# Seven rounds of token routing beside the big products: one scaled running value per token, token-by-expert blocks made once a round, longer gaps

## The chip, the core and the metric

The kernel runs on one core of one Trainium2 chip. The core has a matrix engine (PE, with a second row PEld for its weight loads), a vector engine (DVE), an activation engine (ACT), a general engine (POOL) and a queue that issues DMAs (SP). They run side by side and wait for each other through semaphores; each works through its own instructions in the order in which the program holds them. The metric is the time of one execution on the device in microseconds (us), the median of several runs.

## The reference

Three stages follow each other: a gated linear attention (4 batches, 8 heads, 768 steps, head size 48), a dense layer of 384 to 2048 and back for 3072 tokens, and a routed layer of 8 experts. The change lies in the last one, in the choice of the tokens of each expert:

```
logits = x @ w_gate                       # 3072 tokens x 8 experts
order = np.argsort(-flat)                 # all 24576 pairs, greatest first
for idx in order:
    tok, e = (int(idx) // E, int(idx) % E)
    if assigned[tok] >= 0 or counts[e] >= cap:   # cap = 3072 / 8 = 384
        continue
    assigned[tok] = e; counts[e] += 1
for e in range(E):
    mask = assigned == e
    out[mask] = np.maximum(x[mask] @ w1[e], 0.0) @ w2[e]
```

## The kernel before

The tokens lie as 24 columns of 128. The dense layer is done in groups of three columns: `first` makes `hp` (384 to 2048) and `second` makes `xp` (back to 384). The last three groups' `second` is kept for the end of the program, because the routing needs all logits and these can be had without it: 9 columns of 48 big products, 432 in all, each 128x128 by 128x384, written `xp`. Behind them come 8 experts of 144 big products each: 72 written `hp` (8 blocks of 9) and 72 written `yp` (3 columns of 24). This is `layer2`, the stage of which the change moves the work.

Beside these products runs `route()`. The greedy choice is made in seven rounds, one for each expert that fills up. In a round every token that is still free has its best open expert, and the question is which expert fills first, and at which logit. The logit is turned into a whole number (`key`), and its 32 bits are searched in seven levels, from the top digit down: 5, 5, 5, 5, 4, 4 and 4 bits, that is 32 or 16 thresholds a level. One level is a chain between DVE and PE:

- DVE makes `dg` (the digit plus one), `ge` (token's digit at least each threshold, 768 columns for 32 thresholds, 384 for 16) and `oh` (a block of 128 x 8 x 24: does this token still run, with this expert).
- PE counts, in `c`: `ge` times `oh`, 6 small products for 32 thresholds and 3 for 16. DVE picks the diagonal (`cm`) and sums it (`cd`); PE spreads it over the partitions (`cnt`); DVE compares with the room left (`ok`); PE sums over the experts by powers of two (`tot`); DVE counts the thresholds that some expert still fills (`scr`, with `J`, the digit found, as its running sum).
- With `J` DVE narrows `oh` and `v` to the tokens of that digit, adds to `abv` the tokens above it, and takes their number (`cg`) from the room (`kr`).

In the kernel before, `dg`, `ge` of the next level do not depend on `J`; they are made ahead, `ge` in two halves. Only `scr` and `oh` stand between `tot` and the next `c`.

Behind the seven levels a round has a tail: the expert found is written off, `ps` (two small products) numbers its tokens, and the next round's `m`, `eq0`, `key`, `am`, `oh` and `ge` are made. `token_list` turns the numbers into lists of rows: `ohs`, `h12` and `rh` on DVE, then `pi` and `pj` on PE, then `idx` and `row`, by which POOL gathers the tokens (`xg`) and writes the results (`out`).

The order of the instructions is set in two steps. A driver writes the program: big products advance a clock by their 160 ns each, and a side job runs on when its gap has passed; `GAP` holds the routing's gaps. Then a scheduler of the framework places each engine's instructions by its own costs, so the number of big products between two small ones is not the gap divided by 160. `high_priority` marks the evictions of the big products: `x2` behind `xp` (DVE and ACT), and behind an expert's `hp` the halves `hh` (ACT) and `hl`, in turn on POOL (even blocks) and DVE (odd blocks). All instructions are recorded by one helper, so every row of the trace bears the line L84 and is told by its tile.

Of the kernel before, what the change touches and what calls it, by code (L numbers as in the profile page):

```python
# [9 lines left out]
F32 = mybir.dt.float32  # L10
F16 = mybir.dt.float16
BF16 = mybir.dt.bfloat16
# [79 lines left out]
def body(tc, qk, v, f_logit, w_in, w_out, w_gate, w1, w2, out):  # L92
# [20 lines left out]
    with ExitStack() as ctx:  # L113
# [513 lines left out]
        LEVELS = [(27, 5), (22, 5), (17, 5), (12, 5), (8, 4), (4, 4), (0, 4)]  # L627
        R = {}

        def route_constants():  # L630
# [59 lines left out]

            DVE.tensor_copy(const("opn", [128, E]), wd)
# [13 lines left out]
        def route():  # L705
# [6 lines left out]
            for rnd in range(E - 1):  # L712
# [12 lines left out]
                di = small([128, len(LEVELS), NT], "di", I32)  # L725

                def digit(l):
                    sh, w = LEVELS[l]
                    DVE.tensor_scalar(di[:, l, :], key, sh, 2 ** w - 1, op0=OP.logical_shift_right, op1=OP.bitwise_and)

                def at_least(l):

                    w = LEVELS[l][1]
                    T, G = 2 ** w, 128 >> w
                    dg = small([128, NT], "dg", BF16, 3)
                    DVE.tensor_scalar(dg, di[:, l, :], 1.0, None, op0=OP.add)
                    ge = small([128, NT * 32], "ge", BF16)[:, :NT * T].rearrange("p (a t g) -> p a t g", t=T, g=G)
                    da = dg.rearrange("p (a g) -> p a g", g=G)[:, :, None, :].to_broadcast([128, NT // G, T, G])
                    h = NT // G // 2

                    def part(b):
                        DVE.tensor_tensor(ge[:, b], da[:, b], R[f"thr{w}"][:, b], op=OP.is_ge)

                    return dg, ge, part, (slice(0, h), slice(h, NT // G))

                digit(0)

                oh = small([128, E, NT], "oh", BF16, 3)
                DVE.tensor_tensor(oh, wdx, am[:, None, :].to_broadcast([128, E, NT]), op=OP.is_equal)
                dg, ge, part, halves = at_least(0)  # L750
                part(slice(0, NT // (128 >> LEVELS[0][1])))
                v = small([128, NT], "v", BF16, 3)
                DVE.tensor_tensor(v, dg, un, op=OP.mult)
                kr, abv, cnt, J = kcap, None, None, None
                for l, (sh, w) in enumerate(LEVELS):
                    T, G = 2 ** w, 128 >> w
                    if l > 0:
                        kr, abv = count_above()
# [597 lines left out]
```

## Time and profile before

| what | value |
|---|---|
| three runs | 813.64, 815.62 and 816.38 us, median 815.62 |
| the profiled execution | 822.74 us, its span 820.9 |
| PE busy | 755.0 us (92%), granted clock 0.974 |
| DVE busy | 580.5 us (71%), 1879 instructions |
| ACT, POOL busy | 357.4 us, 142.2 us |

A big product takes a slot of about 0.16 us on PE although its bar is twice as long, since the products are pipelined; so a busy PE hides short waits, and the starts of the instructions say more than the bars. The idle time that a row puts before a product starts at the end of the bar in front of it, some 0.17 us later than the end of that product's slot.

### The profile page before, as it was taken

What the parts mean: (1) busy time and instruction counts of PE and PEld (TensorE: products, weight loads), DVE (VectorE), ACT (ScalarE), POOL (GpSimd) and SP (SyncE); (2) the same over time, 40 slices, a digit from 0 to 9 for tenths busy, and PEclk for the clock granted to TensorE, in tenths of its full rate; (3) what the DMA queues carried; (4) which work ended last, traced back from release to release, by engine and by line L of the source; (5) the groups of instructions that cost most, each with busy time, mean ns of one, the idle gap of its engine ahead of it and who ended that gap; (6) DMA issues with size and microseconds to landing.
All of it is one profiled execution on the core that took longest, in us unless ns stands there. A gap on an engine that the chain in (4) does not pass through costs nothing.

```text
span 820.9 us, 15764 instructions
## 1 busy us (share of the span) xinstructions
PE 755.0 (92%) x5927; PEld 497.6 (61%) x5927; DVE 580.5 (71%) x1879; ACT 357.4 (44%) x748; POOL 142.2 (17%) x140
## 2 busy tenths in 40 slices
PE   6888999899898898989999999999979988989996
PEld 5856776666576565747666666555545545556663
DVE  6799988767975876796673466999899889821310
ACT  6567657655854764583461354000122222213320
POOL 5345311000000000000000000010253443453111
PEclk9699899999999998999999999999999999999998
DMA  9965545698898998996553100040375764744200
GB/s 242 239 155 165 161 128 136 170 276 277 279 270 285 283 296 249 264 324 194 94 96 70 33 1 2 21 174 25 99 239 168 176 182 134 225 155 179 97 30 29
DMA packets 111646, 135.92 MB, mean 166 GB/s; under 512 B 62929, under 2 KB 94674, under 8 KB 109522
## 3 DMA queue, kind: packets, MB, share of 16 engines
q1 hardware_dynamic: 106194, 100.31, 45.2%
q0 software_dynamic: 5376, 34.61, 12.3%
q8 instruction: 46, 0.75, 0.4%
q14 instruction: 30, 0.25, 0.1%
HBM read 86.52 MB, written 34.60 MB: 148 GB/s over the span
## 4 chain that ended last, share of the span: by engine, by line
PE 47%; DVE 24%; DMA 9%; issue 9%; ACT 5%; SPq 5%; POOL 1%; POOLq 0%; ACTq 0%; DVEq 0%
PE hp L84 16%; PE xp L84 13%; DMA xw_s<-in_moe_w 8%; PE yp L84 7%; SPq L84 5%; DVE winu L84 3%; PE y L84 3%; DVE xw_l L84 2%; DVE g L84 2%; PE P L84 2%; DMA fT<-in_f_logit 1%; PE A L84 1%; ACT xw_h L84 1%; PE U L84 1%; DVE woutu L84 1%
## 5 line engine op out<-in xcount | busy, mean ns | idle before, releaser
L84 PE MATMUL hp<-xT,winh 128*128 128x384 f16 x768 | 192.3, 330 | 16.2 <-DVE g L84 16.0
L84 PE MATMUL xp<-wo,gh 128*128 128x384 f16 x768 | 192.1, 328 | 3.1 <-ACT wo L84 2.9
L84 PE MATMUL hp<-xT,winl 128*128 128x384 f16 x384 | 126.6, 330 | 0.0
L84 PE MATMUL xp<-wo,gl 128*128 128x384 f16 x384 | 125.8, 328 | 0.0
L84 PEld LDWEIGHTS <-winh 128*128 128x128 f16 x768 | 74.3, 99 | 64.1 <-issue 24.6
L84 PEld LDWEIGHTS <-gh 128*128 128x128 f16 x912 | 84.2, 98 | 44.4 <-issue 2.9
L84 PE MATMUL hp<-x2T,w1e 128*128 128x384 f16 x576 | 99.7, 325 | 0.8 <-ACT x2T L84 0.6
L84 PE MATMUL yp<-w2e,hh 128*128 128x384 f16 x384 | 95.2, 325 | 0.0
L84 DVE SCALAR_TENSOR_TENSOR xw_l<-xw_s,xw_h 128x768 f16<-128x768 f32 x64 | 61.1, 955 | 46.3 <-ACT xw_h L84 45.8
L84 ACT ACTIVATE g<-hp 128x384 f32<-128x384 f32 x152 | 73.0, 484 | 22.4 <-PE hp L84 20.0
L84 ACT ACTIVATE xw_h<-xw_s 128x768 f16<-128x768 f32 x64 | 53.8, 841 | 65.6 <-DMA xw_s<-in_moe_w 62.7
L84 DVE SCALAR_TENSOR_TENSOR g<-hp,g 128x384 f32<-128x384 f32 x128 | 70.2, 551 | 12.7 <-ACT g L84 12.3
L84 PEld LDWEIGHTS <-w1e 128*128 128x128 f16 x576 | 53.8, 97 | 34.9 <-issue 1.6
L84 PEld LDWEIGHTS <-gl 128*128 128x128 f16 x528 | 48.9, 97 | 31.9 <-issue 4.4
L84 ACT ACTIVATE gh<-g 128x768 f16<-128x768 f32 x64 | 53.8, 841 | 27.4 <-DVE g L84 27.3
L84 DVE TENSOR_TENSOR gl<-g,gh 128x768 f16<-128x768 f32 x52 | 49.7, 955 | 21.5 <-ACT gh L84 21.3
L84 PE MATMUL yp<-w2e,hl 128*128 128x384 f16 x192 | 62.5, 325 | 2.3 <-issue 2.3
L84 POOL IOTA jp<- 128x128 f32 x2 | 0.5, 238 | 369.5 <-PE hp L84 369.4
L84 ACT ACTIVATE hh<-hp 128x384 f16<-128x384 f32 x64 | 31.4, 491 | 72.4 <-PE hp L84 64.3
L84 DVE SCALAR_TENSOR_TENSOR hl<-hp,hh 128x384 f16<-128x384 f32 x40 | 22.1, 553 | 51.6 <-ACT hh L84 49.1
L84 PEld LDWEIGHTS <-winl 128*128 128x128 f16 x384 | 38.0, 99 | 23.2 <-issue 1.4
L84 ACT ACTIVATE x<-yp 128x384 f32<-128x384 f32 x24 | 11.8, 491 | 92.1 <-PE yp L84 89.2
(266 smaller groups left out, 1309.2 us busy)
## 6 DMA issues: line engine op xcount, KB each, us to landing
xw_s<-in_moe_w SPq DMA_DIRECT2D x64, 384.0 KB, 5.3
qkT<-in_qk SPq DMA_DIRECT2D x48, 192.0 KB, 3.6
wout_s<-in_moe_w_out SPq DMA_DIRECT2D x16, 384.0 KB, 3.0
w1d<-xw_h SPq DMA_DIRECT2D x32, 192.0 KB, 3.4
w1d<-xw_l SPq DMA_DIRECT2D x32, 192.0 KB, 4.6
w2d<-xw_h SPq DMA_DIRECT2D x32, 192.0 KB, 4.6
w2d<-xw_l SPq DMA_DIRECT2D x32, 192.0 KB, 4.3
fT<-in_f_logit SPq DMA_DIRECT2D x24, 192.0 KB, 4.2
```

The source lines that it names most:

```text
L84: i = f(*args, **kwargs)
```

## The change

- Levels: 5, 5, 5, 5, 5, 4 and 3 bits with 32, 32, 32, 32, 32, 16 and 16 thresholds, where there were four levels of 32 and three of 16.
- One running value `v` per token takes the place of `oh`, `kr` and `abv` of each level: `v = (v - J) + dg`, with each level's digits scaled by a power of two (`STEP`), so that a token whose digit was above `J` stays above all thresholds of the later levels, and one below stays below. `oh` is made once a round, `ok` compares with `kcap`, and `cg` and `abv` are made once, behind the last level.
- All later digits of a round are made together, in three instructions on blocks of 128 x 144 (`di` shifted, `di` masked, `dg` scaled), instead of two small ones a level.
- `ge` of a level compares `v` with that level's thresholds (`thl1` to `thl6`, made once at the start on DVE, while POOL fills the 18 rows of `sh`, `mk` and `unit`). It now needs `J`, and is one instruction of 768 or 384 columns.
- `GAP` goes from (1000, 500, 500, 700, 1200) to (1500, 700, 600, 700, 2000).

The core of the diff:

```diff
-        LEVELS = [(27, 5), (22, 5), (17, 5), (12, 5), (8, 4), (4, 4), (0, 4)]
+        LEVELS = [(27, 5, 32), (22, 5, 32), (17, 5, 32), (12, 5, 32), (7, 5, 32), (3, 4, 16), (0, 3, 16)]
+        STEP = [2.0 ** (-6 * l) for l in range(len(LEVELS))]
...
+            n = len(LEVELS) - 1
+            sh, mk = (const(x, [128, n, NT], I32) for x in ("sh", "mk"))
+            unit = const("unit", [128, n, NT])
+            for l, (s, w, T) in enumerate(LEVELS[1:]):
+                POOL.memset(sh[:, l, :], s)
+                POOL.memset(mk[:, l, :], 2 ** w - 1)
+                POOL.memset(unit[:, l, :], STEP[l + 1])
+            R["thr"] = [R["thr5"]]
+            for l, (s, w, T) in enumerate(LEVELS):
+                if l > 0:
+                    t = R["thr5" if T == 32 else "thr4"]
+                    u = rc.tile(list(t.shape), BF16, name=f"thl{l}")
+                    DVE.tensor_scalar(u, t, STEP[l], None, op0=OP.mult)
+                    R["thr"].append(u)
+            DVE.tensor_scalar(const("i1s", [128, 16]), R["i1"][:, :16], STEP[-1], None, op0=OP.mult)
...
-                di = small([128, len(LEVELS), NT], "di", I32)
-                def digit(l):
-                    sh, w = LEVELS[l]
-                    DVE.tensor_scalar(di[:, l, :], key, sh, 2 ** w - 1, op0=OP.logical_shift_right, op1=OP.bitwise_and)
-                def at_least(l):
-                    w = LEVELS[l][1]
-                    T, G = 2 ** w, 128 >> w
-                    dg = small([128, NT], "dg", BF16, 3)
-                    DVE.tensor_scalar(dg, di[:, l, :], 1.0, None, op0=OP.add)
+                v = small([128, NT], "v", BF16, 3)
+                d0 = small([128, NT], "d0", I32)
+                DVE.tensor_scalar(d0, key, LEVELS[0][0], 2 ** LEVELS[0][1] - 1, op0=OP.logical_shift_right, op1=OP.bitwise_and)
+                oh = small([128, E, NT], "oh", BF16)
+                DVE.tensor_tensor(oh, wdx, am[:, None, :].to_broadcast([128, E, NT]), op=OP.is_equal)
+                DVE.scalar_tensor_tensor(v, d0, 1.0, un, op0=OP.add, op1=OP.mult)
+                for l, (sh, w, T) in enumerate(LEVELS):
+                    G = 128 // T
                     ge = small([128, NT * 32], "ge", BF16)[:, :NT * T].rearrange("p (a t g) -> p a t g", t=T, g=G)
-                    da = dg.rearrange("p (a g) -> p a g", g=G)[:, :, None, :].to_broadcast([128, NT // G, T, G])
-                    h = NT // G // 2
-                    def part(b):
-                        DVE.tensor_tensor(ge[:, b], da[:, b], R[f"thr{w}"][:, b], op=OP.is_ge)
-                    return dg, ge, part, (slice(0, h), slice(h, NT // G))
-                digit(0)
-                oh = small([128, E, NT], "oh", BF16, 3)
-                DVE.tensor_tensor(oh, wdx, am[:, None, :].to_broadcast([128, E, NT]), op=OP.is_equal)
-                dg, ge, part, halves = at_least(0)
-                part(slice(0, NT // (128 >> LEVELS[0][1])))
-                v = small([128, NT], "v", BF16, 3)
-                DVE.tensor_tensor(v, dg, un, op=OP.mult)
-                kr, abv, cnt, J = kcap, None, None, None
-                for l, (sh, w) in enumerate(LEVELS):
-                    T, G = 2 ** w, 128 >> w
-                    if l > 0:
-                        kr, abv = count_above()
-                    more = l + 1 < len(LEVELS)
-                    if more:
-                        digit(l + 1)
-                        dg2, ge2, part, halves = at_least(l + 1)
+                    va = v.rearrange("p (a g) -> p a g", g=G)[:, :, None, :].to_broadcast([128, NT // G, T, G])
+                    DVE.tensor_tensor(ge, va, R["thr"][l], op=OP.is_ge)
+                    if l == 0:
+                        di = small([128, len(LEVELS) - 1, NT], "di", I32)
+                        DVE.tensor_tensor(di, key[:, None, :].to_broadcast([128, len(LEVELS) - 1, NT]), R["sh"], op=OP.logical_shift_right)
+                        DVE.tensor_tensor(di, di, R["mk"], op=OP.bitwise_and)
+                        dg = small([128, len(LEVELS) - 1, NT], "dg", BF16)
+                        DVE.scalar_tensor_tensor(dg, di, 1.0, R["unit"], op0=OP.add, op1=OP.mult)
                     yield GAP[0] if l else GAP[4]
                     c4 = bank([128, E, G], "c4")
                     for a in range(NT // G):
                         mm(c4, ge[:, a], oh[:, :, a * G:(a + 1) * G], a == 0, a == NT // G - 1)
+                    wt = T.bit_length() - 1
                     cm = small([128, E * 8], "cm", F16)[:, :E * G].rearrange("p (e g) -> p e g", g=G)
-                    DVE.tensor_tensor(cm, c4, R[f"diag{w}"], op=OP.mult)
+                    DVE.tensor_tensor(cm, c4, R[f"diag{wt}"], op=OP.mult)
                     cd = R[f"cd{l % 2}"]
                     with nc.allow_low_precision("one count and zeros"):
                         DVE.tensor_reduce(cd[:, :E], cm, axis=AX.X, op=OP.add)
-                    if more:
-                        part(halves[0])
                     yield GAP[1]
                     cnt = bank([128, 32], "cnt")
-                    mm(cnt[:, :T], cd, R[f"sel{w}"], True, True)
+                    mm(cnt[:, :T], cd, R[f"sel{wt}"], True, True)
                     ok = small([128, 32], "ok", BF16)
-                    DVE.tensor_scalar(ok[:, :T], cnt[:, :T], kr, None, op0=OP.is_ge)
-                    if more:
-                        part(halves[1])
+                    DVE.tensor_scalar(ok[:, :T], cnt[:, :T], kcap, None, op0=OP.is_ge)
                     yield GAP[2]
                     tot = bank([128, 32], "tot")
                     mm(tot[:, :T], R["bits"], ok[:, :T], True, True)
                     J = small([128, 1], "J")
                     scr = small([128, 32], "scr")
-                    DVE.tensor_scalar(scr[:, :T], tot[:, :T], 1.0, None, op0=OP.is_ge, op1=OP.add, accum_out=J)
-                    vp = v
-                    if more:
-                        op = oh
-                        oh = small([128, E, NT], "oh", BF16, 3)
-                        DVE.scalar_tensor_tensor(oh, dg[:, None, :].to_broadcast([128, E, NT]), J, op,
-                                                 op0=OP.is_equal, op1=OP.mult)
-                        dg, ge = dg2, ge2
+                    DVE.tensor_scalar(scr[:, :T], tot[:, :T], STEP[l], None, op0=OP.min, op1=OP.add, accum_out=J)
+                    if l + 1 < len(LEVELS):
+                        vp = v
                         v = small([128, NT], "v", BF16, 3)
-                        DVE.scalar_tensor_tensor(v, vp, J, dg, op0=OP.is_equal, op1=OP.mult)
-                    def count_above(vp=vp, J=J, cnt=cnt, kr=kr, abv=abv, T=T):
-                        cg, k2 = small([128, 1], "cg"), small([128, 1], "kr", F32, 3)
-                        s8 = small([128, 32], "s8")
-                        DVE.scalar_tensor_tensor(s8[:, :T - 1], i1[:, :T - 1], J, cnt[:, 1:T],
-                                                 op0=OP.is_equal, op1=OP.mult, accum_out=cg)
-                        DVE.tensor_tensor(k2, kr, cg, op=OP.subtract)
-                        a2 = small([128, NT], "abv", F32, 3)
-                        if abv is None:
-                            DVE.tensor_scalar(a2, vp, J, None, op0=OP.is_gt)
-                        else:
-                            DVE.scalar_tensor_tensor(a2, vp, J, abv, op0=OP.is_gt, op1=OP.add)
-                        return k2, a2
-                kr, abv = count_above()
+                        DVE.scalar_tensor_tensor(v, vp, J, dg[:, l, :], op0=OP.subtract, op1=OP.add)
+                cg = small([128, 1], "cg")
+                s8 = small([128, 32], "s8")
                 tj = small([128, 1], "tj")
-                DVE.scalar_tensor_tensor(scr[:, :T], i1[:, :T], J, tot[:, :T], op0=OP.is_equal, op1=OP.mult, accum_out=tj)
+                DVE.scalar_tensor_tensor(scr[:, :T], R["i1s"], J, tot[:, :T], op0=OP.is_equal, op1=OP.mult, accum_out=tj)
+                abv = small([128, NT], "abv")
+                DVE.tensor_scalar(abv, v, J, None, op0=OP.is_gt)
                 eqm = small([128, NT], "eqm")
                 DVE.tensor_scalar(eqm, v, J, None, op0=OP.is_equal)
+                DVE.scalar_tensor_tensor(s8[:, :T - 1], R["i1s"][:, :T - 1], J, cnt[:, 1:T],
+                                         op0=OP.is_equal, op1=OP.mult, accum_out=cg)
+                kr = small([128, 1], "kr")
+                DVE.tensor_tensor(kr, kcap, cg, op=OP.subtract)
...
-        GAP = (1000.0, 500.0, 500.0, 700.0, 1200.0)
+        GAP = (1500.0, 700.0, 600.0, 700.0, 2000.0)
```

What the program's order makes of it, in big products between two small ones on PE, counted in the order of both programs:

| from, to | before | after |
|---|---|---|
| start of the kept `xp` to the first `c` | 42 | 55 |
| `c` to `cnt` | mostly 5 (4 to 8) | mostly 4 (4 to 9) |
| `cnt` to `tot` | mostly 3 (3 to 9) | mostly 3 (3 to 7) |
| `tot` to the next `c` | mostly 5 (5 to 9) | 7 to 10 before 32 thresholds, 6 before 16 |
| last `tot` of a round to `ps` | 14, 14, 18, 11, 11, 11, 11 | 11, 11, 16, 11, 14, 14, 11 |
| `ps` to the next round's first `c` | 27, 27, 41, 30, 27, 27 | as below, `c` follows `pi` |
| `ps` to `pi` | 36, 36, 53, 39, 40, 41 | 40, 39, 43, 46, 42, 48 |

The 24 products `xT` that turn the first expert's tokens are counted in the third round. The lists of the rounds come out beside the same experts as before.

On DVE, one whole level in the first round, from one `scr` (the count of thresholds behind `tot`) to the next; before:

```order
L84 TENSOR_SCALAR scr,J<-tot 128x32
L84 SCALAR_TENSOR_TENSOR oh<-dg,J,oh 128x192
L84 SCALAR_TENSOR_TENSOR v<-v,J,dg 128x24
L84 SCALAR_TENSOR_TENSOR s_6445,cg<-i_6231,J,cnt 128x31
L84 SCALAR_TENSOR_TENSOR abv<-v,J,abv 128x24
L84 TENSOR_TENSOR kr<-kr,cg 128x1
L84 TENSOR_TENSOR cm<-c_6461,diag_6268 128x32
L84 TENSOR_SCALAR dg<-di 128x24
L84 TENSOR_REDUCE cd_6303<-cm 128x8
L84 TENSOR_TENSOR ge<-dg,thr_6235 128x128
L84 TENSOR_TENSOR ge<-dg,thr_6235 128x256
L84 TENSOR_SCALAR ok<-cnt,kr 128x32
```

The twelve hold the next level's `ge` in two parts (here for 16 thresholds), outside the way from `scr` to the next `c`. On DVE, a whole level of the changed program's first round, `thl` being the scaled thresholds:

```order
L84 TENSOR_SCALAR scr,J<-tot 128x32
L84 SCALAR_TENSOR_TENSOR v<-v,J,dg 128x24
L84 TENSOR_TENSOR ge<-v,thl_6330 128x768
L84 TENSOR_TENSOR cm<-c_6440,diag_6268 128x32
L84 TENSOR_REDUCE cd_6305<-cm 128x8
L84 TENSOR_SCALAR ok<-cnt,kcap 128x32
```

Six instructions stand where twelve stood, and `ge`, which stood behind `cd`, now stands between `scr` and the `c` that `cm` reads.

On POOL, beside the fifth expert (`hl` are halves of that expert's `hp`, `xg` gathers of later experts' tokens, `out` the results of the expert), before:

```order
L84 TENSOR_TENSOR hl<-g_10145,hh 128x384
L84 DMA xg<-x2d,row 128x768 x6
L84 TENSOR_TENSOR hl<-g_10171,hh 128x384
L84 DMA w1e<-w1d,wi 128x6144
L84 DMA out<-x_10211,idx 3072x384
L84 DMA out<-x_10239,idx 3072x384
```

All six gathers stand in front of an `hl`. On POOL, the same place of the changed program:

```order
L84 TENSOR_TENSOR hl<-g_9676,hh 128x384
L84 TENSOR_TENSOR hl<-g_9702,hh 128x384
L84 DMA w1e<-w1d,wi 128x6144
L84 DMA out<-x_9742,idx 3072x384
L84 DMA xg<-x2d,row 128x768 x6
L84 DMA out<-x_9770,idx 3072x384
```

The six gathers moved from in front of the expert's last `hl` on POOL to behind its first `out`.

## Rows read from the trace of the kernel before

**Rows 1.** View by stretches: us, each engine's busy us (instructions), clock, DMA share, GB/s.
```profile
517.00:591.00 74.00, 72.46 (x569) 42.67 (x568) 66.04 (x442) 4.42 (x9) 5.80 (x6) 1.00 0.21 73
591.00:731.00 140.00, 123.72 (x922) 70.91 (x921) 120.17 (x699) 34.41 (x75) 62.01 (x63) 1.00 0.61 181
```

**Rows 2.** Groups of instructions, PE, 591 to 731: busy us, mean ns | idle before.
```profile
L84 PE MATMUL hp<-x2T,w1e 128*128 128x384 f16 x360 | 64.0, 325 | 0.4 <-ACT x2T L84 0.3
L84 PE MATMUL yp<-w2e,hh 128*128 128x384 f16 x206 | 51.8, 325 | 0.0
L84 PE MATMUL yp<-w2e,hl 128*128 128x384 f16 x102 | 33.1, 325 | 0.0
```

**Rows 3.** Waits of PE, 591 to 731: us in total, times, longest.
```profile
PE pi L84 <- DVE rh L84: 3.8, 5, 1.0
PE c L84 <- DVE oh L84: 3.0, 4, 1.0
PE cnt L84 <- DVE cd L84: 2.8, 4, 1.2
PE tot L84 <- DVE ok L84: 2.0, 3, 1.1
```

**Rows 4.** Waits of PE, 517 to 591.
```profile
PE c L84 <- DVE oh L84: 0.7, 2, 0.4
```

**Rows 5.** Timeline of PE, one level of the first round: start us, us.
```profile
526.21 0.18 PE L84 MATMUL cnt<-sel,cd 128*128 128x32 f16 x1
...
526.74 0.18 PE L84 MATMUL tot<-ok,bits 128*128 128x32 bf16 x1
...
527.67 0.20 PE L84 MATMUL c<-oh,ge 128*128 128x32 bf16 x2
```

**Rows 6.** Timeline of DVE, the same level.
```profile
526.96 0.19 DVE L84 TENSOR_SCALAR_CACHE_REDUCE scr<-tot 128x32 f32<-128x32 f32 x1 [0.28 <-PE tot L84]
...
527.20 0.42 DVE L84 SCALAR_TENSOR_TENSOR oh<-dg,J,oh 128x192 bf16<-128x192 bf16 x1
...
528.08 0.18 DVE L84 TENSOR_TENSOR cm<-c,diag 128x32 f16<-128x32 f32 x1
```

**Rows 7.** Groups of instructions, DVE, 517 to 731.
```profile
L84 DVE TENSOR_TENSOR ge<-dg,thr 128x384 bf16<-128x384 bf16 x42 | 14.1, 348 | 0.0
L84 DVE SCALAR_TENSOR_TENSOR hl<-hp,hh 128x384 f16<-128x384 f32 x20 | 11.0, 548 | 2.5 <-issue 2.4
...
L84 DVE SCALAR_TENSOR_TENSOR v<-v,J,dg 128x24 bf16<-128x24 bf16 x42 | 9.9, 237 | 0.0
...
L84 DVE TENSOR_TENSOR ge<-dg,thr 128x768 bf16<-128x768 bf16 x7 | 3.8, 549 | 0.0
...
L84 DVE TENSOR_TENSOR lg<-lg,es 128x192 f32<-128x192 f32 x7 | 2.5, 358 | 0.0
```

**Rows 8.** Timeline of PE, tail of the fourth round.
```profile
652.26 0.18 PE L84 MATMUL ps<-x,ones 128*128 128x48 bf16 x1
...
652.96 3.90 PE L84 MATMUL hp<-x2T,w1e 128*128 128x384 f16 x23
...
660.90 0.42 PE L84 MATMUL pi<-rh,ohs 128*128 128x96 bf16 x6 [0.58 <-DVE rh L84]
```

**Rows 9.** Timeline of POOL, the same tail.
```profile
655.58 1.34 POOL L84 TENSOR_TENSOR hl<-g,hh 128x384 f16<-128x384 f32 x1 [1.20 <-ACT g L84]
```

**Rows 10.** Timeline of DVE, the same tail.
```profile
656.03 0.92 DVE L84 TENSOR_SCALAR un<-asg 128x24 f32<-128x24 f32 x1
```

**Rows 11.** Timeline of POOL, beside the fifth expert.
```profile
730.41 0.92 POOL L84 TENSOR_TENSOR hl<-g,hh 128x384 f16<-128x384 f32 x1
```

**Rows 12.** Timeline of PE, the same place.
```profile
731.39 0.34 PE L84 MATMUL yp<-w2e,hl 128*128 128x384 f16 x1 [2.25 <-issue]
```

**Rows 13.** Timeline of DVE, start of the routing.
```profile
519.08 0.55 DVE L84 TENSOR_TENSOR ge<-dg,thr 128x768 bf16<-128x768 bf16 x1
```

**Rows 14.** Timeline of PE, the same place.
```profile
519.75 0.31 PE L84 MATMUL c<-oh,ge 128*128 128x32 bf16 x6
```

## The prediction

> **What bounds the kernel now.** I read the busy shares by slice first, to find the stretch that the change touches: from 511 us on, the kept `xp` products and then the experts. The view by stretches shows a DVE there that is as loaded as PE while the routing runs, 66.0 of 74 us and then 120.2 of 140 us [rows 1]. PE's own busy time says little, so the reader should count its products. The 23 `hp` of a tail last 3.90 us, the last bar 0.33 of it, so a slot is (3.90 - 0.33) / 22 = 0.162 us [rows 8]. In 591 to 731 PE runs 360 + 206 + 102 = 668 big products [rows 2], 108.5 us. The small ones follow each other at about 0.025 us (two `c` last 0.20, and one bar of such a size is 0.18 [rows 5]) and come to some 8 us, an estimate by their number. The rest of the 140 us, 23.5, is waiting. The view of waits says for what: `pi` for `rh`, `c` for `oh`, `cnt` for `cd`, `tot` for `ok`, all of DVE [rows 3]. Beside `xp` it names only 0.7 us [rows 4]. So PE's queue sets the end, and what can be won is its waits for DVE; 2.25 us of them are another thing, a `yp` that waits for the `hl` that POOL begins at 730.41 behind six gathers [rows 11, 12].
>
> **The level.** A clean level before: `tot` at 526.74, `scr` 0.22 later, `oh` 0.24 behind that (the running sum is read out first), 0.42 us of `oh`, and `c` 0.05 behind its end, at 527.67: 0.93 us [rows 5, 6]. The five products between fill 0.025 + 5 x 0.162 = 0.84, so PE waits 0.09. That is 42 x 0.09, about 4 us in seven rounds, too small for the view of waits.
> After, the way is `scr`, `v`, `ge`, `c`. `v` keeps its form, 0.24 us; `ge` of 768 columns has 0.55, of 384 columns 0.35 [rows 7]. A dependent instruction starts about 0.04 behind the end of its forerunner, as `scr` behind the 0.18 of `tot` [rows 5, 6]. So 0.22 + 0.24 + 0.24 + 0.04 + 0.55 + 0.05 = 1.34 us before 32 thresholds, 1.14 before 16. Seven products fill 1.16, six fill 1.00: waits of 0.18 and 0.14. The order has 21 sevens and 13 sixes there; the other eight steps have eight to thirteen products and wait about nothing. 21 x 0.18 + 13 x 0.14 = 5.6 us. From `c` to `cnt`: `cm` starts 0.41 behind the first of six `c` [rows 5, 6], then 0.18 + 0.04 for `cm`, about the same for `cd`, 0.05 to PE: 0.87 us. Six `c` and four products fill 0.80, where five filled 0.96: 49 x 0.07 = 3.4 us that were not there. Together 9 against 4: the level **loses 5 us**, although half of its DVE instructions go. The chain has grown by more than the added products fill.
>
> **Start, and more `c`.** The new constants and larger blocks stand on DVE ahead of the first `c`. `ge` began at 519.08 and ended 0.55 later, `c` began at 519.75 [rows 13, 14], so nothing was spare; the order now gives 13 more products, 2.1 us. Four `thl` of 768 columns and two of 384 have no row: from above `ge` of the same sizes, which has two inputs and not one, 2.9 us; from below half of that, since rows of fewer columns get shorter, 1.4. An `x2` eviction (its form is that of `hl`, 0.55), and `di` twice and `dg` once on 144 columns (nearest `lg` with 192, 0.36, so about 0.27 each; from below `v`, 0.24 [rows 7]) add 1.3, less 0.2 for what they replace. 2.5 to 4.0 against 2.1 gives 0.4 to 1.9, and down to 0 if they overlap as neighbours do; I take **+1**. 21 more `c` at 0.025 are **+0.5**.
>
> **The tails beside `xp`.** Between `ps` and `rh` DVE drops four small instructions and the two halves of a `ge` (0.27 each from start to start, from its 0.35), and gains `di` twice, `dg` and an eviction: about +0.2 us, and `place` in the first round, against three or four more products but now without the earlier stop at `c`. **+0.5** over two rounds, 0 to 2.
>
> **The tails beside the experts.** Before, in the fourth round, `ps` stands at 652.26 and `pi` at 660.90 [rows 8]: 8.64 us over 36 products, some 6.1 with the small ones. 2.5 us of waiting, in two steps. Part of it is POOL's: `un` takes 0.92 us and ends with the `hl` that POOL began at 655.58 [rows 9, 10], where `v` on as many columns has 0.24. So a POOL `hl` that meets such an instruction costs DVE about 0.7 us, and two do in this tail.
> The Trainium skill (SBUF — State Buffer, Who interferes with whom) says that VectorE and GpSimd share a port pair which is locked for a whole instruction, and that a VectorE instruction with two SBUF inputs contends with a GpSimd one that reads SBUF. `un` beside `hl` agrees; by that rule a hold can last the whole 0.92 of an `hl` [rows 11], and two holds in four tails would add 4 x 2 x 0.2 = 1.6 us to the sum.
> After, the tail lies deeper in the `hp` products: one more DVE `hl` inside and one ahead of `totc` (0.47 each from start to start, an estimate from 0.55), and 0.25 for the blocks of 144 less the `ge` halves. 8.64 + 0.94 + 0.25 = 9.8 us with the same two POOL `hl`, over 42 to 48 products, 6.9 to 7.9: waits of 1.9 to 2.9, now once a round. 2.4 in four rounds and 0.3 in the last: 10 us. What stands behind the tail (`cnt`, `tot`, the next `c`) waited too, since DVE was still behind; afterwards a level leaves DVE time to catch up, and I leave 3 us, from 1 to 6. Before, tails and what follows had 23.5 - 2.25 - 26 x 0.09 = 18.9; after 13: **-5.9**.
>
> **POOL.** The gathers stand behind the last `hl` and the first `out` now and are wanted an expert later, so the wait of `yp` goes: **-2.3**; if it came back at the next expert's `hl`, 0.
>
> **Sum.** +5 + 1 + 0.5 + 0.5 - 5.9 - 2.3 = -1.2 us. The profiled execution took 822.74 us, 7 over the median; the sum is a difference and is put on the median of the runs: 815.6 - 1.2 = **814.4 us**. 0.3%, 2.4 us, is about what this measurement can tell from no change.
>
> **Rivals.** *DVE's relief decides* (faster). A level drops six of twelve instructions, and DVE is busy 120.2 of 140 us [rows 1]. If `cnt` and `tot` never wait again (4.8 us [rows 3]) and the tails halve their other 14, with `yp`'s 2.3, that is -14; the level's +5 and +2 for start and `c` stay: 815.6 - 7 = 808.6. For it speaks DVE's load; against it, that the tail, where `pi` and `c` wait, loses little work.
> The Trainium skill (VectorE: DVE Perf Modes, Rules for kernel authors) advises to minimise the count of operations in a chain. By it this rival would be right; the rows count less for the number than for the way from `tot` to `c`, which gets longer.
> *The chain takes over* (slower). Place: `tot` to `c`. DVE's evictions, 20 `hl` [rows 7] and nine of `xp`, go through the same queue. Where one falls between `scr` and `ge`, or a POOL `hl` holds `ge`, the chain is 0.47 to 0.7 longer, and nothing else on DVE's side can be done ahead any more. If 20 of them do so, 20 x 0.47 = 9.4 us: 823.8. It decides from a third of them on, when `tot` to `c` is often over 1.5 us.
> *The lists come late.* The last ones end some 30 products later in the fifth expert, but are wanted an expert later, 144 products or 23 us; I give it nothing.
>
> **Numbers.** Forecast case 0.42 (811 to 818), relief 0.34 (805 to 812), chain 0.24 (817 to 826). Faster by over 0.3%: 0.07 of the first and 0.31 of the second, 0.38. Slower: 0.02 and 0.22, 0.24. Within: 0.38. The range of 806 to 822 leaves out the ends of both rivals.
>
> **What would show it.** `tot` to `c` near 1.34 and 1.14 us and `c` to `cnt` near 0.87; often over 1.5 would be the chain. One wait of 1.9 to 2.9 us at `pi` in each tail beside the experts, almost none at `c` behind it; under 1 would be the relief. No wait of `yp` for POOL near the end of the routing. The first `c` 2 to 4 us later than 519.75. DVE busy in the experts' stretch well under 120 us. The account would be wrong if the waits of that stretch fell under 12 us or rose over 28.

## The result and the profile after

The changed kernel took 827.8 us (median of 4 runs, 821.5 to 830.6) and the kernel before, run beside it, 816.0 (4 runs): a ratio of 1.0126, 95% interval 1.0077 to 1.0175. In a second comparison with twelve runs it was 829.3 us and 1.0073 (1.0034 to 1.0112). I had forecast 814.4 us and no difference. **It is slower, by about 0.7 to 1.3%.**

The two programs are the same up to the 721st `xp` product, the first of the last three groups, and this part ends anywhere between 501.9 and 515.7 us in the nineteen profiles taken for this study, whichever kernel ran. So I compare the *stage* that begins with that product, in three stretches: beside `xp` (to the first expert's first `hp`), four experts (to the fifth's first `hp`), and the rest. It is 310.0 us in the profile before, 82.0 + 118.5 + 109.4 (each rounded). These are the stretches of the profile after, by start and end; the columns are as in [rows 1]:

```profile
505.77:589.79 84.02, 81.63 (x643) 45.65 (x640) 63.66 (x349) 5.08 (x12) 7.78 (x8) 1.00 0.19 68
589.79:710.19 120.40, 109.05 (x801) 59.86 (x801) 91.34 (x437) 27.93 (x61) 49.24 (x49) 0.97 0.62 183
710.19:819.07 108.88, 98.41 (x642) 58.96 (x641) 32.23 (x117) 27.62 (x59) 30.78 (x32) 0.98 0.32 109
```

313.3 us, 3.3 more: two beside `xp`, two beside the four experts, and half a microsecond back in the rest. DVE is relieved as the diff says, but PE gained nothing from it. What PE waits for in 512 to 586 (the first row) and 586 to 726, against [rows 3, 4]:

```profile
PE pi L84 <- DVE rh L84: 1.2, 2, 0.7
...
PE pi L84 <- DVE rh L84: 10.0, 4, 3.1
PE ps L84 <- DVE x L84: 2.1, 4, 0.7
PE c L84 <- DVE ge L84: 0.3, 1, 0.3
```

The waits for `cnt` and `tot` have left this view and those for `c` nearly so; four waits at `pi` hold nearly as much as the four kinds did together (10.0 us of 11.6). The level that answers to [rows 5, 6], first on PE:

```profile
518.80 0.18 PE L84 MATMUL tot<-ok,bits 128*128 128x32 bf16 x1
...
520.15 0.32 PE L84 MATMUL c<-oh,ge 128*128 128x32 bf16 x6
```

and on DVE:

```profile
519.02 0.19 DVE L84 TENSOR_SCALAR_CACHE_REDUCE scr<-tot 128x32 f32<-128x32 f32 x1 [0.28 <-PE tot L84]
...
519.26 0.24 DVE L84 SCALAR_TENSOR_TENSOR v<-v,J,dg 128x24 bf16<-128x24 bf16 x1
519.54 0.56 DVE L84 TENSOR_TENSOR ge<-v,thl 128x768 bf16<-128x768 bf16 x1
520.50 0.19 DVE L84 TENSOR_TENSOR cm<-c,diag 128x32 f16<-128x32 f32 x1 [0.41 <-PE c L84]
```

`tot` to `c` is 1.35 us. The tail that answers to [rows 8 to 10], on PE, then DVE, then POOL:

```profile
625.12 0.18 PE L84 MATMUL ps<-x,ones 128*128 128x48 bf16 x1 [0.54 <-DVE x L84]
...
625.17 7.64 PE L84 MATMUL hp<-x2T,w1e 128*128 128x384 f16 x46
634.93 0.42 PE L84 MATMUL pi<-rh,ohs 128*128 128x96 bf16 x6 [2.12 <-DVE rh L84]
```

```profile
627.71 0.92 DVE L84 TENSOR_TENSOR s<-s,x 128x48 f32<-128x48 f32 x1
...
631.06 0.55 DVE L84 TENSOR_TENSOR ge<-v,thr 128x768 bf16<-128x768 bf16 x1
631.53 0.91 DVE L84 TENSOR_SCALAR si<-sl 128x24 int32<-128x24 f32 x1
632.47 0.18 DVE L84 TENSOR_SCALAR lo<-si 128x24 int32<-128x24 int32 x1
...
634.60 0.28 DVE L84 TENSOR_SCALAR rh<-h,pcol 128x288 bf16<-128x288 bf16 x1
```

```profile
627.63 0.93 POOL L84 TENSOR_TENSOR hl<-g,hh 128x384 f16<-128x384 f32 x1 [1.59 <-ACT g L84]
630.54 1.86 POOL L84 TENSOR_TENSOR hl<-g,hh 128x384 f16<-128x384 f32 x1 [1.98 <-ACT g L84]
```

PE does 46 products and stands 2.1 us. DVE has no gap from 628.5 to 634.9, and two of its instructions on 24 or 48 columns last 0.9 us, to the end of a POOL `hl`. Behind the longest wait, 3.1 us at 603.03, the products themselves are slow; the granted clock is the seventh number:

```profile
604.00:607.00 3.00, 3.00 (x14) 1.45 (x13) 1.85 (x11) 0.87 (x2) 1.32 (x2) 0.50 0.34 66
```

0.50 is the 1.2 GHz level: the big products follow each other at 0.32 us there in place of 0.16. Counted over PE's starts (a slot of 0.162 us, as in the prediction; this finds 3.3 us where the view has 3.1), ten products are slow behind that wait and nine behind one of 2.5 us, and they lose 2.75 us; in the profile before none does.

### The profile page after: what moved, and what is told of

Same layout as the page of the kernel before. It is cut to its first block, busy times and chain, and to the rows that moved or that the text cites. A ratio compares the mean times of both kernels' runs of the same rounds, so it can differ in the third digit from the quotient of the medians.

```text
span 819.1 us, 15511 instructions
## 1 busy us (share of the span) xinstructions
PE 756.6 (92%) x5948; PEld 493.7 (60%) x5948; DVE 561.0 (68%) x1564; ACT 357.3 (44%) x748; POOL 142.7 (17%) x158
## 3 DMA queue, kind: packets, MB, share of 16 engines
q0 software_dynamic: 5376, 34.61, 12.1%
## 4 chain that ended last, share of the span: by engine, by line
PE 50%; DVE 21%; DMA 11%; issue 8%; ACT 5%; SPq 4%; POOL 1%; POOLq 0%; ACTq 0%; DVEq 0%
PE hp L84 16%; PE xp L84 15%; PE yp L84 8%; DMA xw_s<-in_moe_w 8%; SPq L84 4%; PE y L84 3%; DVE winu L84 2%; DVE xw_l L84 2%; DVE g L84 2%; PE c L84 2%; ACT xw_h L84 1%; PE A L84 1%; PE U L84 1%; PE P L84 1%; DMA fT<-in_f_logit 1%
## 5 line engine op out<-in xcount | busy, mean ns | idle before, releaser
L84 ACT ACTIVATE x<-xp 128x384 f16<-128x384 f32 x24 | 11.7, 487 | 94.0 <-PE xp L84 82.1
```

Source lines behind the costliest of these rows:

```text
L84: i = f(*args, **kwargs)
```

## The experiments

The kernels of a numbered set ran on the same chip and share the runs of the kernel before; another set ran on another chip. Stage times are from one profile each:

| kernel | beside xp | four experts | rest | stage | ratio of times to before (95%) |
|---|---|---|---|---|---|
| 1: before, again | 82.1 | 119.4 | 109.4 | 310.9 | 1.0030 (0.9998 to 1.0062) |
| 1: after, again | 83.9 | 120.2 | 111.0 | 315.1 | 1.0073 (1.0034 to 1.0112) |
| 1: after, old gaps | 84.1 | 118.4 | 108.6 | 311.1 | 1.0014 (0.9980 to 1.0047) |
| 1: before, new gaps | 81.8 | 121.9 | 108.8 | 312.5 | 1.0003 (0.9972 to 1.0033) |
| 2: after, later constants | 82.8 | 120.1 | 108.9 | 311.7 | 1.0031 (0.9998 to 1.0064) |
| 2: after, later pi | 83.3 | 117.7 | 108.2 | 309.3 | 1.0038 (1.0004 to 1.0073) |
| 2: after, both | 83.0 | 119.1 | 108.2 | 310.2 | 0.9965 (0.9938 to 0.9991) |
| 2: after, PE kept busy | 85.6 | 120.4 | 111.0 | 317.0 | 1.0144 (1.0089 to 1.0199) |
| 3: after, no hl on POOL | 83.9 | 110.9 | 110.9 | 305.7 | 0.9953 (0.9921 to 0.9985) |
| 3: before, no hl on POOL | 81.5 | 109.4 | 109.5 | 300.4 | 0.9884 (0.9831 to 0.9937) |
| 3: both of 2, no hl on POOL | 83.1 | 112.0 | 111.8 | 306.8 | 0.9904 (0.9865 to 0.9942) |
| 3: old gaps, later constants | 82.5 | 117.2 | 108.6 | 308.3 | 0.9969 (0.9929 to 1.0010) |
| 4: before, no hl on POOL | 81.4 | 104.1 | 107.1 | 292.6 | 0.9800 (0.9764 to 0.9836) |
| 4: old gaps, later constants, no hl on POOL | 82.4 | 106.0 | 107.8 | 296.3 | 0.9842 (0.9797 to 0.9888) |
| 4: the same, digits later | 82.5 | 106.8 | 107.4 | 296.7 | 0.9851 (0.9810 to 0.9893) |
| 5: before, no hl on POOL | 81.4 | 104.2 | 107.1 | 292.7 | 0.9816 (0.9772 to 0.9860) |
| 5: after, no hl on POOL | 83.7 | 106.4 | 108.2 | 298.3 | 0.9885 (0.9844 to 0.9926) |

**1. Where does the loss lie, and in which half of the change?** Both kernels again, and each with the other's gaps:

```
-        GAP = (1500.0, 700.0, 600.0, 700.0, 2000.0)
+        GAP = (1000.0, 500.0, 500.0, 700.0, 1200.0)
```

> The changed kernel once more, unchanged. The two profiles put the stage from the first kept xp to the end at 313.3 us, before 310.0; the part ahead of it is the same program. Theory S: ratio 1.004 to 1.008, 3 to 7 us, with the stage at 313 to 317. Theory L: the 1.0126 of the first comparison came mostly from the part ahead of the stage; ratio 1.004 (3.3 us) here, stage 313 again. If the ratio is 1.012 again and the stage 313, the changed program makes the part ahead slower, though its order there is the same.

> The changed kernel with the old gaps (1000, 500, 500, 700, 1200) alone: running value and blocks as changed, fewer big products between. If the chain from tot to c decides, PE waits 0.3 to 0.5 us more at each of 42 steps and the time rises by 10 us or more over the changed kernel. If the tail decides (pi waits for rh 2.3 to 3.3 us in four rounds), the gaps of the levels matter less, rounds get shorter and it comes out within 4 us of the changed kernel.

> The kernel before with the new gaps alone. If the longer gaps shift the tails into the hp products and that is the loss, it is slower than before by 3 to 8 us, with pi waits of 2 us and more. If the running value is the loss, it is like before or faster by up to 4 us, since its level chain is shorter and gets more cover.

The loss is there again and lies in the stage: 4.2 us in this pair of profiles, 2.1 of them one `hp` in the rest that waited for ACT, which the other profile of the changed kernel doesn't have. The new value costs 2 us beside `xp` with either set of gaps, so that part isn't the gaps'. Beside the four experts it is: the new gaps cost 2.5 to 3.4 us on the old value and 1.8 to 2.0 on the new one, by the profiles. The run times agree for the new value, which with the old gaps is 8.5 us faster in this set, more than the 4 foretold. For the old value their interval (1.0003, 0.9972 to 1.0033) doesn't show it. TensorE's clock falls there too: in the kernel before with the new gaps it is 0.50 from 603 to 608 us, so that cost belongs to the gaps and not to the new value. With the old gaps `c` comes ahead of `pi`, and PE stands there:

```profile
PE c L84 <- DVE ge L84: 8.9, 8, 1.9
PE ps L84 <- DVE x L84: 1.8, 1, 1.8
PE pi L84 <- DVE rh L84: 1.6, 2, 1.1
```

The wait follows whichever product is first to need DVE.

**2. The constants.** In the profile after, the new constants stand on DVE ahead of the first search, and POOL's 18 fills are followed by `zeros`, which ends at 506.32:

```profile
504.97 1.38 DVE L84 TENSOR_SCALAR i<-i 128x32 f32<-128x32 f32 x1
...
512.43 1.48 DVE L84 TENSOR_SCALAR thl<-thr 128x768 bf16<-128x768 bf16 x6
```

```profile
505.58 0.74 POOL L84 MEMSET zeros<- 128x768 bf16 x1
```

`i` ends 0.04 us behind `zeros`. It took 0.77 us in the second profile of the kernel before, where POOL only fills `zeros` there. The edit moves the fills to DVE, behind the first `ge`, and each `thl` behind a count of the first round:

```
-                POOL.memset(sh[:, l, :], s)
+                DVE.memset(R["sh"][:, l, :], s)
...
+                    if rnd == 0 and l + 1 < len(LEVELS):
+                        thresholds(l + 1)
```

> The changed kernel, with its new constants made later: the 18 fills of shifts, masks and units go from POOL to DVE and behind the first round's first ge, and each scaled threshold block is made on DVE behind the count of the level before. Everything behind the first round stands in the same order. The stage is taken from the first product of the last three groups' gate columns (the 721st xp) to the end: 310.0 and 311.0 us in the two profiles of the kernel before, 313.3 in the profile after. Theory C (about 2 us of the loss come from the constants): in the trace after, the six scaled blocks and i1s stand on DVE ahead of the first search, 1.5 us more than before between bits and opn, POOL's fills hold three DVE instructions for 1.3 us in place of 0.7, and PE waits 0.71 us at lp. Without them the first c comes some 9 us behind the stage's start (11.6 after, 8.9 before), the wait at lp is gone, the stretch beside the xp products is 82 to 82.5 us in place of 84.0, and the stage 311 to 312. Rival W (it only moves the work): the blocks now delay the first round's own levels by 6 x 0.27 us and more, its c waits grow by as much, the stretch stays at 84 and the stage at 313.

Theory C holds in the main: 82.8 us beside `xp` (82 to 82.5 foretold), stage 311.7, the first `c` 8.9 us behind the stage's start, the wait at `lp` gone, and `i` at 0.50. Which part the fills have in it and which the blocks isn't separated. The first `i`:

```profile
505.38 0.50 DVE L84 TENSOR_SCALAR i<-i 128x32 f32<-128x32 f32 x1
```

**3. More products in the tails.** The gaps put 38 products ahead of the tail's `c`, and `pi` behind it. The levels get their old gaps with the same edit.

```
-        GAP = (1500.0, 700.0, 600.0, 700.0, 2000.0)
+        GAP = (1000.0, 500.0, 500.0, 700.0, 7000.0)
...
-            yield 600.0
+            yield 7500.0
             pi = bank([128, 24, G], "pi")
```

> The changed kernel with other gaps alone: GAP (1000, 500, 500, 700, 7000), and the list's last yield ahead of pi 7500 in place of 600. PE's order then has 38 big products between ps and the next round's first c, and pi some 16 behind that c, where after has 42 to 48 and then pi, c directly behind it. Theory P (the loss beside the experts is PE standing at pi, 2.3 to 3.3 us in each of four tails, and its clock at 1.2 GHz for some products afterwards, 2.8 us in all): pi waits under 0.5 us, the first c waits under 1.0, no product has half the clock, and the stretch from the first experts' product to the fifth expert's is 111 to 114 us where it is 118.6 before and 120.4 after; the stage 304 to 307. Rival D (DVE's own chain is the bound, whatever stands between): what pi no longer waits for, c, cnt and tot wait for; the stretch stays at 118 to 120 and the stage at 312 or more.

> Both edits on the changed kernel: the later constants and the later pi. If both theories hold the gains add up: the stage 302 to 305 us, the time 8 to 10 us under that of the changed kernel and 5 to 7 under the kernel before. If theory C falls it is as a_later alone; if theory P falls, 311 and no faster than before.

Theory P falls for the most part. `pi` no longer waits, `c` and `cnt` do:

```profile
PE c L84 <- DVE ge L84: 4.6, 5, 1.6
PE cnt L84 <- DVE cd L84: 4.4, 4, 1.8
```

117.7 us beside the experts is close to rival D's 118 to 120, though the stage of 309.3 is better than its 312. The slow products aren't all gone either: the granted clock is 0.50 from 694 to 697 us. Both edits together have a stage of 310.2 us, where 302 to 305 was foretold; in time they beat the kernel before by 0.1 to 0.6%. The later `pi` gave nothing of its own that is clear: against the changed kernel with the old gaps the stage is 1.8 us shorter with it, and with the later constants in both (set 3) 1.9 us longer.

**4. PE kept busy.** 24 products that do nothing ahead of `pi`.

> The changed kernel with 24 small products of 96 columns (0.043 us each, 1.03 us) that do no work, issued on PE directly ahead of each list's pi; they read the last two operands that are made before rh, so they run while PE would wait for rh. Their result is overwritten. Theory K (the clock drops because PE stood still): in after the ten products behind the wait of 3.31 us and the nine behind that of 2.52 go at 1.2 GHz, 0.32 us each in place of 0.16, 2.8 us in all; here PE stands still for 1 to 2 us at most at these places, as in the kernel before where no product goes at half the clock, and the big products behind pi keep 0.16 us; the stage is 2 to 3 us shorter than after's 313.3. Rival N (the drop has another cause): the products behind pi still go at 1.2 GHz in some tails, and the stage is the same or 1 us longer.

Half of theory K holds. Of the 2.75 us in slow products 0.27 are left, where the second profile of the changed kernel has some 1.3; this speaks for a clock that fell because PE stood. But the four experts take 120.4 us as in the profile after, and the stage is 3.7 us longer where 2 to 3 less was foretold. The added products have a part in that. They can start only with `h`, last 1 us, and end behind `rh`:

```profile
606.04 1.18 PE L84 MATMUL pi<-h,ohs 128*128 128x96 bf16 x24 [1.13 <-DVE h L84]
607.06 0.42 PE L84 MATMUL pi<-rh,ohs 128*128 128x96 bf16 x6
```

```profile
606.25 0.29 DVE L84 TENSOR_SCALAR rh<-h,pcol 128x288 bf16<-128x288 bf16 x1
```

`pi` starts 0.2 to 1.4 us behind the end of `rh` in the four tails beside the experts, where it was 0.05 in the profile after: 2.4 us in all, as much as the clock gave back. Beside `xp`, where `pi` waited 0.7 us at most, the added products lengthen the stretch by 1.6 us, and the rest by 2.1. So this run doesn't show what the slow clock costs.

**5. POOL holds DVE.** Every `hl` on DVE, in three kernels.

```
-                    if f % 2 == 0 and r < E - 2:
+                    if False:
```

> The changed kernel with every hl on DVE: of the 24 hl of each of the first six experts none is subtracted on POOL any more, and ACT's second copy of the ones that were goes too. In the trace after, 16 POOL subtractions lie beside the tails' stretch (589.8 to 710.2), and 13 DVE instructions there last over 0.3 us longer than the shortest of their form, 9.2 us together (si 0.91 in place of 0.17, rh 0.94 in place of 0.28 in one tail); DVE gets 16 hl of 0.55 us in exchange, 8.8 us. Theory H (what makes PE stand in the tails is DVE held by POOL, since the held instructions lie on the chain to rh): the waits at pi fall from 2.3 to 3.3 us by 0.7 to 1.4 each, and the experts' stretch from 120.4 to some 117; si, un and rh go at 0.17 to 0.28 us throughout. Rival X (the exchange is even): the hl on DVE take the same time from the same chain, the waits stay within 0.5 us and the stretch at 119 to 121.

(POOL does 24 `hl` in all, four for each of the first six experts, and not 24 for each.)

> The kernel before with the same edit, every hl on DVE. The same 13 held instructions, 10.1 us, are in its trace. Under theory H its experts' stretch falls as well, from 118.6 to 119.4 to some 116, because its oh, ge and cd lie on the same chain; under rival X it stays, or grows by 1 to 3 us, since DVE has 120 of 140 us busy there and 8.8 us of hl more with less room than the changed kernel's.

Theory H, and more than it said: 9 to 10 us off the four experts in either kernel, and some 14 in sets 4 and 5. The kernel before with this one edit is the fastest of all: 802.2 and 801.6 us. No DVE instruction of the stage lasts over 0.3 us longer than the shortest of its form any more, where 13 did beside four experts before (10.1 us) and after (9.2 us). What the hold costs a tail is seen best in two tails of the changed kernel that have nearly the same number of big products on PE, 42 and 43, and two `hl` of DVE's own each. With `hl` on POOL:

```profile
655.84 0.18 PE L84 MATMUL ps<-x,ones 128*128 128x48 bf16 x1 [0.18 <-DVE x L84]
...
665.23 0.64 PE L84 MATMUL pi<-rh,ohs 128*128 128x96 bf16 x6 [2.35 <-DVE rh L84]
```

```profile
656.74 0.76 DVE L84 TENSOR_TENSOR_SCAN inc<-ones,totc 128x48 f32<-128x48 bf16 x1
...
660.07 0.91 DVE L84 TENSOR_SCALAR un<-asg 128x24 f32<-128x24 f32 x1
...
662.89 0.77 DVE L84 TENSOR_SCALAR hi<-si 128x24 int32<-128x24 int32 x1
```

and with every `hl` on DVE (set 5):

```profile
653.82 0.18 PE L84 MATMUL ps<-x,ones 128*128 128x48 bf16 x1
...
661.42 0.42 PE L84 MATMUL pi<-rh,ohs 128*128 128x96 bf16 x6 [0.41 <-DVE rh L84]
```

```profile
655.19 0.25 DVE L84 TENSOR_TENSOR_SCAN inc<-ones,totc 128x48 f32<-128x48 bf16 x1
...
658.38 0.17 DVE L84 TENSOR_SCALAR un<-asg 128x24 f32<-128x24 f32 x1
...
658.95 0.17 DVE L84 TENSOR_SCALAR hi<-si 128x24 int32<-128x24 int32 x1
```

From `ps` to `pi` it is 9.39 us in the one and 7.60 in the other, 1.8 less; the three held instructions are 1.85 us shorter.

The edit does more than take the hold away, though. The scheduler sets the routing wider with it: from one `ps` to the next beside the experts PE has 155 to 162 big products in the kernel before, where it had 141 to 145, and 162 to 168 in the changed one, where it had 147 to 153. So PE has more to do while DVE works, and how much of the 14 us comes from this isn't separated. 2.3 us in the rest of the kernel before are the wait of `yp` for POOL's `hl`, which goes too. ACT's relief was not run by itself; in the profile before no wait of DVE that its view names beside the four experts is for ACT.

In the kernel before, the same groups of DVE, 517 to 731, were:

```profile
L84 DVE TENSOR_SCALAR rh<-h,pcol 128x288 bf16<-128x288 bf16 x8 | 3.6, 450 | 0.0
L84 DVE TENSOR_SCALAR un<-asg 128x24 f32<-128x24 f32 x7 | 2.9, 411 | 0.0
```

and in the changed kernel of set 5, 512 to 726, with twice the `hl`:

```profile
L84 DVE SCALAR_TENSOR_TENSOR hl<-hp,hh 128x384 f16<-128x384 f32 x41 | 22.7, 554 | 3.6 <-ACT hh L84 3.1
...
L84 DVE TENSOR_SCALAR rh<-h,pcol 128x288 bf16<-128x288 bf16 x8 | 2.3, 290 | 0.0
L84 DVE TENSOR_SCALAR un<-asg 128x24 f32<-128x24 f32 x7 | 1.2, 168 | 0.0
```

The Trainium skill (Perfetto Trace Analysis, Optimizing Scalar/DVE Operations) says that shifting work between GpSimd and VectorE might not help, since they share a port. The traces agree and go further here: shifting it back, with the wider order that comes with it, makes the kernel before 1.2% (set 3) to 2.0% (set 4) faster.

**6. What is the change worth without the hold?**

> The later constants, the later pi and every hl on DVE, on the changed kernel. In a_best two instructions of a tail are held, un 0.90 and rh 0.94 us, and PE stands 0.6 to 1.7 us at c and 1.9 to 2.0 at cnt behind them. Under theory H those cnt waits go, and the stage is 304 to 307 us where a_best has 310.2; under rival X it is 309 to 311.

> The changed kernel with the old gaps and the later constants. If what was seen adds up (the old gaps 2.2 us on the stage of 313.3, the later constants 1.6) the stage is 309.5 us, within 1 us of a_best, and the time 1 to 3 us under the kernel before. If the later pi matters by itself, it is 1.5 us or more behind a_best.

> The kernel before with every hl on DVE, a second time: its stage was 300.4 us in one profile, 9.6 to 10.5 under the kernel before, and its time is based on four runs. Theory H says the same again: stage 300 to 302, time 8 to 10 us under the kernel before.

> The changed kernel with the old gaps, the later constants and every hl on DVE. Theory V (once the three losses are taken out, that is the constants, the gaps and POOL's hold, the search's shorter DVE work is worth something): a_og_const has a stage of 308.3 us where the kernel before has 310.0 to 311.0, so with the hold gone it is 298 to 300, under b_nopool's 300.4, and the time 1 to 3 us under b_nopool's. Rival E (DVE's 38 us of saved work lie in slots where PE waited for nothing): the stage is 300 to 303 and the time that of b_nopool within 2 us.

> As a_ogc_nopool, and the three instructions on all 144 lower digits of a round (di, di, dg, 0.9 us of DVE) are issued behind the count of the round's first level in place of ahead of it. They stand between the round's end and the first c in the traces so far. Theory V2 (the tail is DVE's chain, so 0.9 us less in it counts): the first c of each round waits 0.5 us less, the stage is 2 to 3 us under a_ogc_nopool. Rival E2 (without POOL's hold the chain no longer ends last in the tails): the same within 1 us.

> The changed kernel with every hl on DVE, a second time, beside b_nopool_3. Under rival E (the search's saved DVE work lies where PE waits for nothing) the change costs here what its constants and gaps cost, 2 to 5 us over b_nopool_3. Under theory V (they only cover a gain) it is within 1 us of it or faster.

The old gaps and later constants add up (308.3 us, 309.5 expected), and with the hold in place that is 1.7 to 2.6 us under the kernel before, with a time that can't be told from its own (0.9929 to 1.0010): gaps and constants account for the loss there. It is also 1.9 us under both edits of set 2, so the later `pi` doesn't matter by itself. Both edits of set 2 without `hl` on POOL have 306.8 us, at the upper end of theory H's 304 to 307. With old gaps, later constants and `hl` off POOL, the changed kernel comes to 296.3, under theory V's 298 to 300, but the kernel before to 292.7, where 300 to 302 was foretold: V falls. In set 5, side by side, the changed kernel takes 806.8 us to 801.6, 5.2 more where rival E had 2 to 5, and its stage is 5.6 us longer. PE's waits by kind (the longest row of each view, 589.0 to 713.4 in the changed kernel, 583.4 to 705.6 in the kernel before) are small in both:

```profile
PE pi L84 <- DVE rh L84: 1.7, 4, 0.6
```

```profile
PE ps L84 <- DVE x L84: 0.3, 1, 0.3
```

What is left is below this view. Counted over PE's starts in the whole stage, PE waits 17.1 us in the one and 12.1 in the other: 3.1 of the difference at `pi`, 0.7 at `lp`, 0.7 at `c`, 1.0 at `cnt`. With the old gaps and the later constants it is 15.1, and 3.4 us more at `c` than in the kernel before without `hl` on POOL are more than all of the difference. Issuing the digits later changes nothing (rival E2). So I read it as rival E does: DVE's saved work lay where PE waited for nothing, and the longer way to `c` costs. E's stage of 300 to 303 was too long.

One thing stays open. The kernel before without `hl` on POOL had 300.4 us in set 3 and 292.6 and 292.7 later, with the same order on PE. So had the changed one, 305.7 and then 298.3. The profiles of set 3 have waits of 1.0 to 2.1 us that the later ones lack. I don't know their cause (the chip was another one), and compare sets 4 and 5.

## Why the prediction was wrong

- **The level (+5): right.** `tot` to `c` is 1.35 us (1.34 foretold), and 1.15 before 16 thresholds (1.14). `c` to `cnt` is 0.83, not 0.87. The waits under 0.35 us at `c`, counted over PE's starts, sum to 7.2 us where before had 3.0; those at `cnt` come to 1.6 in all, half of the 3.4 foretold, and before had 1.0 there already.
- **Start, more `c`, tails beside `xp` (+2): the sum right, the share wrong.** The stretch grew by 2.0 us, but three of seven rounds' share of the level was in it too. The first `c` is 2.75 us later, within the 2 to 4 named. The 18 fills on POOL I gave nothing; they hold DVE 0.6 us longer, and PE 0.7 at `lp`.
- **The tails beside the experts (-5.9): this is the step that failed.** The stop at `pi` came as foretold, 2.1 to 3.1 us in each of four tails, 10.0 in total in the view of waits (10 foretold). What was wrong is the 3 us left for all that stands "behind the tail". Counted over PE's starts, the four experts have 20.6 us of waits, 10.8 at `pi` and 4.0 at `c`, mostly the level's; 5.8 are behind and around the tails, 2.75 of them products at 1.2 GHz, which the prediction put at nothing. From 586 to 726, which answers to the prediction's 591 to 731, all waits but the level's come to some 18 us, where it had 13, and 18.9 before: the term is about -1. The stretch grew by 1.9 us, 1.4 of them waits, in place of falling by some 3. (The tail of [rows 8] is the fifth of that table and has 40 big products, not 36, so that it waits 2.0 us and not 2.5. The 9.8 us worked out for a tail of the changed kernel fits all the same: 9.4 to 10.5.)
- **POOL (-2.3): a quarter of it.** The `yp` wait is gone, but `ps`, `pi` and `c` wait 3.1 us in the rest where `ps` and `pi` had 1.8, and it is 0.5 us shorter.
- **The rivals.** "The chain takes over" had the sign, not the mechanism: `tot` to `c` didn't grow by evictions. "DVE's relief decides" fails where I put its weakness, in the tail. What lengthens the tail in both kernels is neither: it is POOL's hold of DVE, which I had priced at 0.7 us twice a tail and then left alone, as a cost that the two kernels share. Shared it is, and it doesn't set the two apart: without it the changed kernel is still 5.2 us slower. The old order stood the hold in several waits, mostly up to 1.3 us (2.3 once in the second profile), at full clock, the new one in a single wait of 2.3 to 3.3 us a tail (counted over PE's starts). `un`, which the prediction set beside the rule on two SBUF inputs, reads one block: its row shows a hold, and not that rule.
- **The account.** Stage +3.3 and +4.2 us in two pairs of profiles; outside the span +0.5 (2.3 to 2.4 us, 1.8 before). The second comparison's 6.0 us (2.8 to 9.2) covers that. The first one's 10 us is more, and the part ahead of the stage, which varies by itself, is the likely place of it: with one slope of span on mean clock for all runs of the first comparison and of sets 1 to 3 with `hl` on POOL (5 to 6 us for 0.01), the changed kernel's span is some 5 us over that of the kernel before (about 4 to 6).

## What to carry to other kernels

Before shortening an engine's work, look at which of its instructions the bound engine really waits for, and whether these last longer than the shortest of their form: here a neighbour's instructions held them, and moving 24 subtractions, with the order that came of it, won 15 to 16 us (sets 4 and 5) where the whole change lost 6 to 10. A chain that got longer by one dependent instruction lost a little on most levels, although half of the work went. And waits gathered into one place by longer gaps cost 1.8 to 3.4 us more beside the experts, by the profiles, than the same work with the waits in pieces.

## What the runs showed of the hardware

- A POOL subtraction of 128x384 f32 holds a DVE instruction to its end: 13 of them, of 1 to 288 columns, beside 16 subtractions, in the profile before and in the one after. `si` took 0.91 us for 0.17, `rh` 0.94 for 0.28 (beside the later `pi`). POOL's fills do so too (`i`, which lasts until `zeros` ends, 0.50, 0.77 and 1.38). POOL's indirect DMA issues, 64 in the stage, didn't: with them alone there, no DVE instruction lasted over 0.3 us longer than the shortest of its form.
- TensorE fell to 1.2 GHz for ten and nine products after standing 3.3 and 2.5 us (counted over PE's starts), with little work between, but not after every wait of that size: a second one of 2.5 us had none behind it in the same profile, and in the second profile of the changed kernel only the wait of 3.3 us had nine. It fell in the kernel before with the new gaps as well.
- The time outside the span was 1.8 us before and 2.3 to 2.4 in the changed kernel. Without its fills on POOL it was 1.9 to 2.0, and with the fills but without `hl` on POOL 1.8 again (medians); what sets it stays open.
